# First loads cut finer, a first tile turned in halves, and a transpose queue and a TensorE order set anew

## The chip, the cores and the metric

One core of a Trainium2 chip runs the whole program. The metric is the time on the device in microseconds; lower is better. Several runs of a kernel are given as their median.

## The reference

The input x has 2048 tokens of width 448. It is normalised per token, and two branches run on the result. One is attention with a feature map: q, k and v for 16 heads of width 28, a small matrix w_phi per head, softmax of the plus and of the minus product as features, then keys times values summed over all tokens. The other is a dense pair with silu between. Both are added to x.

```python
xn = _layernorm(x, axis=-1)
qkv = (xn @ wqkv)                                # 448 -> 3*448, 16 heads of 28
pq, pk = q @ w_phi, k @ w_phi                    # per head, 28 x 28
phi = concat(softmax(p), softmax(-p))            # 56 features, for q and for k
kv, z = phi_k^T @ v, sum(phi_k)                  # over all 2048 tokens
attn = ((phi_q @ kv) / (phi_q @ z + 1e-6)) @ wo
ffn = silu(xn @ w1) @ w2                         # 448 -> 1792 -> 448
out = x + attn + ffn
```

## The kernel before

The program is a list of operations (`P.op`, `P.dma`), each with an engine, an estimated length, and what it reads and writes. `schedule` (line 218) is a planner: it simulates the engines with these estimates and fixes the order of instructions on each engine. `chain` (line 869) adds order by name where the author wants one, and the words of `PLAN` (line 334) fix TensorE's order from the fourth FFN1 block on: each word hangs on the one before. What an instruction truly waits for at run time is only its data, by semaphores.

Tokens are 16 tiles of 128. For each tile `ln_tile` (line 596) issues on VectorE the statistics (`bnst`, `bnag`), the inverse deviation (`rstd`, with a square root `ve` on ScalarE for tiles 0 to 3 and on GpSimd for the others), and the normalised tile (`xn`). Tiles 0 to 3 are turned over by four TensorE transposes each (`tr`) and evicted to `xnT` (`ev`, ScalarE for 0 to 2, VectorE for 3). Tiles 4 to 15 are turned over by DMA, two tiles at a time (`xnT_dma5`, `xnT_dma7` and so on), issued from SyncE.

The weights of q and k are folded with w_phi on the chip. Eight DMA transposes (`wT_dma0` to `wT_dma7`) bring wqkv into `wT_sb` (in the profile Y_sb, whose memory it shares), GpSimd spreads w_phi to a block diagonal (`bdphi`), and the two words f0 and f2 multiply them, each for two of four row slices. Every f word reads all eight transposes.

SyncE issues all loads in order and then the transposes: x tile 0, x tile 1, x tiles 2 and 3, w1 columns 0 to 511 and 512 to 1023 (each as three row groups and a remainder), x tiles 4 to 7, the rest of w1, wv, x tiles 8 to 11, x tiles 12 to 15, then the chain at line 910, then w2 and wo. ScalarE issues w_phi as its first instruction. `w1_sb` lies in `phT` in the profile, xn and phq in RA, the attention outputs in vaug.

The head of TensorE's order is 38 warm-up matmuls, the transposes of tiles 0 to 3, and FFN1 blocks F0, F1 and F2 (256 columns of w1 each) for tokens 0 to 511, tile by tile with 128-row matmuls (`part`). Blocks after that are done as two halves with 64-row matmuls side by side: in `PLAN` aF3@4 is the first half of FFN1 block 3 in banks 4 and 5, bF3 its second half and eviction; v, k, q are the projections of a pair of tiles. F7 and above need tiles 4 to 7. K is keys times values, Y and F with a colon are FFN2 steps of a tile, U the attention product, W, R, r and E the product with wo and the output. The kernel's own estimates list a clash of 225 ns where a half follows the other half on the same bank, and 95 ns for a switch between 64 and 128 rows.

Of the kernel before, what the change touches and what calls it, by code (L numbers as in the profile page):

```python
# [140 lines left out]
class _Prog:  # L141
# [68 lines left out]
    def dma(self, fn, xfer, reads=(), writes=(), name="", out_slot=None, eng="sp", issue=480.0, lat=1700.0):  # L210
        o = self.op(eng, issue, fn, reads, writes, name=name)
        o.is_dma = True
        o.xfer = xfer
        o.lat = lat
        o.out_slot = out_slot
        return o

    def schedule(self):
# [21 lines left out]
        eng_free = {e: 800.0 if e == "sp" else 0.0 for e in ENGINES}  # L240
# [93 lines left out]
PLAN = """aF3@4 aF4@0 bF3 aF5@2 av2@6 bF4 bv2 bF5 aF6@0 bF6 av0@4 bv0 aF7@0 aF8@2 aF10@4 bF8 bF10 bF7 f2@26 aF11@4 aF13@0 bF11  # L334
bF13 f0@26 aF9@4 aF12@0 bF9 av4@2 ak0@6 bv4 bF12 bk0 av6@4 av8@2 ak4@0 bv8 bk4 bv6 av14@6 ak2@2 bv14 bk2 av12@0 ak6@4
bv12 bk6 ak8@6 av10@2 ak10@0 bv10 bk10 bk8 ak12@2 ak14@4 bk12 bk14 aq4@0 Y0@6:3 Y0:2 K0-6 bq4 aq6@4 K6-8 bq6 aq0@2 aq8@0
bq0 bq8 aF15@4 Y0:9 K8-12 bF15 aF19@2 aF14@0 bF19 bF14 aF17@5 s4 aF18@3 bF17 bF18 K12-16 aF16@5 aF21@2 aF24@0 bF21 bF16
bF24 M s6 aF27@2 aF26@4 bF27 aF22@0 bF26 bF22 aF20@6 aq2@2 bF20 aF23@0 aF25@4 bF23 bF25 bq2 U4 s8 F4@1:10 U9@0 s0 aq12@6
aq14@4 aq10@2 s2 bq12 bq10 bq14 F4:3 F4:1 F9@0:10 F8@3:3 F8:3 s10 W4 U8 s12 F8:6 Y1@4:14 F9:4 W9 U2 U0@5 F2@2:6 F2:8
F8:2 U7@6 U12@5 W8 Y3@4:9 Y3:5 W2 s14 W0@5 F7@4:9 F7:1 U1 F7:4 W7 R0,2 R8,7 R4,9 F10@6:5 U6@5 U10 F10:9 U3@3 F5@4:14  # L340
U13@2 F15@51:8 U15 F15:6 F12@2:5 F12:9 U14 F6@0:5 W12 E15 U5 F13@3:11 F6:9 F14@7:5 F13:2 F13:1 U11@1 W5 W3@5 r12 W13
F14:9 W14 r14 W6 W1@2 W10 R3,6,13,1,5,10 F11@1:7 F11:6 F11:1 W11 r11"""


def bass_parallel_sum__linear_kernel_hedgehog__dense_activation_silu__prompt_kernel(
# [30 lines left out]
    with es:  # L376
# [157 lines left out]
        def load_rows4(dst, src, c0, c1, name, lat=1700.0):  # L534
            load(dst[:, 0:3, :], src[0:KF, c0:c1].rearrange("(k p) f -> p k f", p=128), name, lat=lat)
            load(dst[:, 3, :], src[D - 128:D, c0:c1], name, lat=lat)

        def load_w1(c0, c1, lat=1700.0):
            load_rows4(w1_sb[:, :, c0:c1], B_w1, c0, c1, "w1", lat)

        load(Wp[:], A_w_phi.rearrange("(g hl) d f -> (hl d) g f", g=G), "wphi", eng="act", lat=3000.0)
# [15 lines left out]
        def dma_t(dst, src, xfer, name, issue=1235.0, **kw):  # L557
            o = P.dma(lambda e: e.dma_start_transpose(out=dst, in_=src), xfer, lat=650.0, reads=[src] if kw.pop("sbuf", True) else [],
                      writes=[dst], name=name, issue=issue if xfer < 1500.0 else 2000.0, **kw)
# [36 lines left out]
        def ln_tile(t):  # L596
# [16 lines left out]
            def norm(dst, c0, c1, dur):  # L613
                P.op("dve", dur, lambda e: e.tensor_scalar(dst, x_sb[:, t, c0:c1], mv[:, t, 0:1], rstd[:, t:t + 1], ALU.subtract, ALU.mult),  # L614
                     reads=[xs, mv[:, t, 0:1], rstd[:, t:t + 1]], writes=[dst], name=f"xn{t}")
# [488 lines left out]
```

The softmax here doesn't subtract the row's maximum and nothing guards it: scores larger than these inputs give would overflow.

## Time and profile before

| | |
|---|---|
| median of the runs | 151.64 us (4 runs, 151.1 to 152.54) |
| profiled execution, own time | 151.12 us |
| its span, first to last instruction | 149.4 us |
| granted TensorE clock | 1.00 |
| TensorE busy | 143.9 us, 96% of the span |
| VectorE, ScalarE, GpSimd busy | 91.3, 70.2 and 70.9 us |
| first FFN1 matmul | starts at 7.05 us |
| first fold | starts at 26.28 us |
| last matmul work ends, last store lands | about 146.6 us, about 149 us |

Times in the views count from the start of the span. PE is TensorE's matmuls, PEld its weight loads, DVE VectorE, ACT ScalarE, POOL GpSimd, SP SyncE; SPq and ACTq are instructions that only issue a DMA. L468 is the helper that records every matmul, L488 the one of every ScalarE activation, so those groups are told apart by the tiles they write and read.

### The profile page before, as it was taken

To read this page: it belongs to the slowest core of one execution; us is meant where nothing else is said; L and a number is where in the kernel's file an instruction comes from. 1 tells how busy PE (TensorE), PEld (TensorE's weight loads), DVE (VectorE), ACT (ScalarE), POOL (GpSimd) and SP (SyncE) were. 2 spreads that over 40 slices of the span, in tenths; PEclk is the share of its full clock that TensorE was granted. 3 is DMA by queue.
4 is the path that set the end of the run, shared out by engine and by line. 5 is a ranking of instruction groups with operands and counts; after the bars stand their busy time and mean duration, and the time that the engine had idled before them with its cause. 6 is when DMAs were issued, how large, how long until landed. Compare 5 with 4: busy or idle time off the path is not lost.

```text
span 149.4 us, 3406 instructions
## 1 busy us (share of the span) xinstructions
PE 143.9 (96%) x1412; PEld 79.0 (53%) x1412; DVE 91.3 (61%) x186; ACT 70.2 (47%) x86; POOL 70.9 (47%) x82
## 2 busy tenths in 40 slices
PE   7699999999999999999999999999999999999992
PEld 7494434555555565454544445455555566655540
DVE  1968998850198999212995028897542974334263
ACT  3467764547999997965475495910000000000000
POOL 7208568210049999999699900999600000000000
PEclk9999999999999999999999999999999999999999
DMA  5999976999300000000099594079968645140224
GB/s 87 306 375 367 183 135 117 191 232 347 101 0 4 0 4 4 0 4 0 0 105 181 99 181 75 0 140 174 122 130 162 172 101 107 36 100 4 68 92 154
DMA packets 44352, 17.41 MB, mean 117 GB/s; under 512 B 36784, under 2 KB 43952, under 8 KB 44336
## 3 DMA queue, kind: packets, MB, share of 16 engines
q1 hardware_dynamic: 41568, 15.36, 48.1%
q10 hardware_dynamic: 2768, 1.83, 3.8%
q8 instruction: 11, 0.18, 0.5%
q14 instruction: 5, 0.04, 0.1%
HBM read 6.56 MB, written 1.84 MB: 56 GB/s over the span
## 4 chain that ended last, share of the span: by engine, by line
PE 93%; DMA 3%; SPq 1%; DVE 0%; issue 0%
PE psum L468 93%; DMA phT<-in_B_w_dram 3%; SPq L529 1%; DVE x_sb L842 0%; PE psum L483 0%
## 5 line engine op out<-in xcount | busy, mean ns | idle before, releaser
L468 PE MATMUL psum<-xnT,phT 64*128 64x512 bf16 (+1 forms) x428 | 45.1, 350 | 0.9 <-DMA phT<-in_B_w_dram 0.8
L468 PE MATMUL psum<-w_sb,hT 128*128 128x448 bf16 (+1 forms) x238 | 45.4, 342 | 0.0
L488 ACT ACTIVATE hT<-psum 128x1024 bf16<-128x1024 f32 x28 | 27.4, 1023 | 18.0 <-PE psum L468 18.0
L728 DVE TENSOR_REDUCE Rec<-Ek_sb 128x32 f32<-128x896 bf16 (+1 forms) x20 | 24.3, 1247 | 13.7 <-ACT Ek_sb L488 7.9
L468 PEld LDWEIGHTS psum<-xnT,phT 64*128 64x128 bf16 (+1 forms) x428 | 20.9, 95 | 21.5 <-ACT xnT L488 0.9
L468 PEld LDWEIGHTS psum<-w_sb,hT 128*128 128x128 bf16 x238 | 21.6, 98 | 19.0 <-issue 1.5
L763 POOL TENSOR_TENSOR RA<-Ek_sb,Rec 128x896 bf16<-128x896 bf16 x16 | 26.6, 1699 | 9.1 <-ACT Ek_sb L488 7.8
L468 PE MATMUL psum<-Wqk,xnT 64*128 64x432 bf16 x224 | 22.9, 343 | 0.0
L488 ACT ACTIVATE Ek_sb<-psum 128x864 bf16<-128x864 f32 x24 | 20.3, 934 | 2.9 <-issue 2.7
L738 POOL TENSOR_TENSOR Ek_sb<-Ek_sb,Rec 128x896 bf16<-128x896 bf16 x8 | 13.3, 1695 | 11.2 <-DVE Rec L729 11.2
L820 DVE TENSOR_SCALAR den<-psum 128x16 f32<-128x16 f32 x16 | 2.5, 162 | 22.3 <-PE psum L468 22.3
L468 PEld LDWEIGHTS psum<-Wqk,xnT 64*128 64x128 bf16 x224 | 10.6, 94 | 9.5 <-ACT Ek_sb L488 0.2
L738 POOL TENSOR_TENSOR phT<-phT,Rec 128x896 bf16<-128x896 bf16 x8 | 13.3, 1697 | 0.0
L468 PE MATMUL psum<-wv,xnT 64*128 64x448 bf16 x112 | 12.9, 349 | 0.1
L599 DVE BATCH_NORM_STATS2 st<-x_sb 128x6 f32<-128x448 bf16 x16 | 9.7, 605 | 3.9 <-DMA x_sb<-in_A_x_dram 3.8
L614 DVE TENSOR_SCALAR RA<-x_sb,mv,rstd 128x384 bf16<-128x384 bf16 (+2 forms) x28 | 10.6, 417 | 1.3 <-POOL rstd L610 1.2
L468 PE MATMUL psum<-wo_sb,vaug 128*128 128x448 bf16 (+2 forms) x51 | 11.0, 341 | 0.0
L827 DVE TENSOR_TENSOR vaug<-psum,rden 128x448 bf16<-128x448 f32 x16 | 9.9, 624 | 0.4
L842 DVE TENSOR_TENSOR x_sb<-psum,x_sb 128x448 bf16<-128x448 f32 (+2 forms) x14 | 7.6, 585 | 3.8 <-PE psum L468 3.8
L729 DVE RECIPROCAL Rec<-Rec 128x32 f32<-128x32 f32 (+1 forms) x24 | 8.6, 393 | 0.1
L468 PEld LDWEIGHTS psum<-wv,xnT 64*128 64x128 bf16 x112 | 5.4, 94 | 5.6 <-PE psum L468 0.5
L488 ACT ACTIVATE vaug<-psum 128x896 bf16<-128x896 f32 x8 | 7.4, 947 | 1.6 <-PE psum L468 1.6
(49 smaller groups left out, 102.8 us busy)
## 6 DMA issues: line engine op xcount, KB each, us to landing
out_dram<-x_sb ACTq DMA_DIRECT2D x15, 112.0 KB, 1.7
w_sb<-in_B_w_dram SPq DMA_DIRECT2D x1, 1568.0 KB, 7.8
x_sb<-in_A_x_dram SPq DMA_DIRECT2D x3, 448.0 KB, 7.5
phT<-in_B_w_dram SPq DMA_DIRECT2D x2, 384.0 KB, 4.9
wo_sb<-in_A_wo_dram SPq DMA_DIRECT2D x2, 336.0 KB, 8.9
phT<-in_B_w_dram SPq DMA_DIRECT2D x1, 576.0 KB, 6.8
wv<-in_A_wqkv_dram SPq DMA_DIRECT2D x1, 336.0 KB, 7.1
phT<-in_B_w_dram SPq DMA_DIRECT2D x2, 128.0 KB, 4.8
```

Of the source, the lines that this page charges most:

```text
L468: r = e.matmul(dst, lhsT, rhs, start=st, stop=sp, skip_group_check=True)
L488: P.op("act", d_act(n), lambda e: e.activation(dst, src, func, scale=scale), reads=[src], writes=[dst], table=table, name=name, **keys)
L529: P.dma(lambda e: e.dma_start(out=dst, in_=src), n / 280.0, writes=[dst], name=name, eng=eng, lat=lat)
L599: P.op("dve", 590, lambda e: e.bn_stats(st6[:, t, :], xs), reads=[xs], writes=[st6[:, t, :]], name=f"bnst{t}", okeys_w=["ln"])
L614: P.op("dve", dur, lambda e: e.tensor_scalar(dst, x_sb[:, t, c0:c1], mv[:, t, 0:1], rstd[:, t:t + 1], ALU.subtract, ALU.mult), reads=[xs, ...
L728: P.op("dve", 50 + 967 * n, lambda e: e.tensor_reduce(R2, E4, AXL.X, ALU.add), reads=[E4], writes=[R2], name="Ssum")
L729: P.op("dve", 135 + 210 * n, lambda e: e.reciprocal(R2, R2), reads=[R2], writes=[R2], name="Rrec")
L738: P.op("pool", 1700, lambda e: e.tensor_tensor(E3, E3, Rk[:, :, None].broadcast_to([128, 32, DH]), ALU.mult), reads=[E3, Rk], writes=[E3], ...
L763: P.op("pool", 1700, lambda e: e.tensor_tensor(dst, Eq, Rq.rearrange("p (c j) -> p c j", c=CC)[:, :, :, None].broadcast_to([128, CC, 4, DH ...
L820: P.op("dve", 190, lambda e: e.tensor_scalar(den[:, uq, :], U3[:, :, DH], EPS_DEN, None, ALU.add), reads=[U3[:, :, DH]], writes=[den[:, uq ...
L827: P.op("dve", 620, lambda e: e.tensor_tensor(o3, U3[:, :, 0:DH], rden[:, uq, :, None].broadcast_to([128, H, DH]), ALU.mult), reads=[U3[:, ...
L842: P.op("dve", d_dve(cs.stop - cs.start), lambda e: e.tensor_tensor(res[:, cs], ob, addend[:, cs], ALU.add), reads=[ob, addend[:, cs]], wri ...
```

## The change

- w1 comes in pieces of 256, 256, 256, 512 and 512 columns in place of 512, 512 and 768. The first piece is issued by ScalarE, after its first activation (`warm_act`); the others by SyncE. w_phi moves from ScalarE's first place to SyncE's queue, behind x tiles 12 to 15.
- Tile 0 is normalised in two parts (256 and 192 columns), transposed in two parts, and evicted in two parts. F0 and F1 take the first two row slices of tile 0 before the third, and F2 comes before tile 1.
- On SyncE's queue x tiles 12 to 15 and w_phi stand behind `xnT_dma5`, and `wT_dma3` to `wT_dma7` stand behind `xnT_dma7`.
- GpSimd's two memsets of the ones column wait for the last normalisation (xn15) in place of following rstd15 in order.
- The planner's estimates for DMA issue and transfer change, and `PLAN` has a new order of the same blocks. In its first line aF6 and aF5 come before the v blocks, bF4 follows bF3, f0 comes before f2, and aF8 stands ahead of bv0.

```diff
-    def dma(self, fn, xfer, reads=(), writes=(), name="", out_slot=None, eng="sp", issue=480.0, lat=1700.0):
+    def dma(self, fn, xfer, reads=(), writes=(), name="", out_slot=None, eng="sp", issue=520.0, lat=1700.0):
...
-        eng_free = {e: 800.0 if e == "sp" else 0.0 for e in ENGINES}
+        eng_free = {"sp": 800.0, "act": 2550.0, "pe": 0.0, "dve": 0.0, "pool": 0.0}
...
-PLAN = """aF3@4 aF4@0 bF3 aF5@2 av2@6 bF4 bv2 bF5 aF6@0 bF6 av0@4 bv0 aF7@0 aF8@2 aF10@4 bF8 bF10 bF7 f2@26 aF11@4 aF13@0 bF11
-bF13 f0@26 aF9@4 aF12@0 bF9 av4@2 ak0@6 bv4 bF12 bk0 av6@4 av8@2 ak4@0 bv8 bk4 bv6 av14@6 ak2@2 bv14 bk2 av12@0 ak6@4
...
+PLAN = """aF3@4 aF4@0 bF3 bF4 aF6@6 aF5@2 bF6 bF5 av2@4 bv2 av0@6 aF8@2 aF7@0 bF8 aF10@4 bv0 bF10 bF7 f0@26 aF11@4 aF13@0 bF11
+bF13 f2@26 aF9@4 aF12@0 bF9 av4@2 ak0@6 bv4 bF12 bk0 av8@2 av6@4 ak4@0 bv8 bk4 bv6 av14@6 ak2@2 bv14 bk2 av12@0 ak6@4
...
-        def load_rows4(dst, src, c0, c1, name, lat=1700.0):
-            load(dst[:, 0:3, :], src[0:KF, c0:c1].rearrange("(k p) f -> p k f", p=128), name, lat=lat)
-            load(dst[:, 3, :], src[D - 128:D, c0:c1], name, lat=lat)
-
-        def load_w1(c0, c1, lat=1700.0):
-            load_rows4(w1_sb[:, :, c0:c1], B_w1, c0, c1, "w1", lat)
-
-        load(Wp[:], A_w_phi.rearrange("(g hl) d f -> (hl d) g f", g=G), "wphi", eng="act", lat=3000.0)
+        def load_rows4(dst, src, c0, c1, name, eng="sp"):
+            load(dst[:, 0:3, :], src[0:KF, c0:c1].rearrange("(k p) f -> p k f", p=128), name, eng)
+            load(dst[:, 3, :], src[D - 128:D, c0:c1], name + "r", eng)
+
+        def load_w1(c0, c1, eng="sp"):
+            load_rows4(w1_sb[:, :, c0:c1], B_w1, c0, c1, f"w1_{c0}", eng)
+
         load_x(0, 1)
         load_x(1, 2)
         load_x(2, 4)
-        load_w1(0, 512)
-        load_w1(512, 1024)
+        load_w1(0, 256, "act")
+        load_w1(256, 512)
+        load_w1(512, 768)
         load_x(4, 8)
-        load_w1(1024, FF)
+        load_w1(768, 1280)
+        load_w1(1280, FF)
         load_rows4(wv_sb, A_wqkv, 2 * D, 3 * D, "wv")
         load_x(8, 12)
         load_x(12, 16)
+        load(Wp[:], A_w_phi.rearrange("(g hl) d f -> (hl d) g f", g=G), "wphi", lat=2500.0)
...
-                dma_t(wT_sb[:, a, :], A_wqkv[:, a * KP:a * KP + 128], 600.0, f"wT_dma{a}", (1600.0, 1400.0, 1780.0, 3280.0)[a] if a < 4 else 1300.0, sbuf=False)
+                dma_t(wT_sb[:, a, :], A_wqkv[:, a * KP:a * KP + 128], 600.0, f"wT_dma{a}", 1800.0 if a == 2 else 1310.0, sbuf=False)
...
                 if t % 2:
                     dma_t(xnT[:, t - 1:t + 1, :, :].rearrange("p i k c -> p (i k) c"),
-                          xn_sb[:, sl - 1:sl + 1, :].rearrange("p i c -> p (i c)"), 1300.0, f"xnT_dma{t}", 1350.0)
+                          xn_sb[:, sl - 1:sl + 1, :].rearrange("p i c -> p (i c)"), 2200.0 if t < 8 else 1600.0, f"xnT_dma{t}", 1350.0)
                 return
-            tps = bank16[4 + t % 2][:, 0:512].rearrange("p (k c) -> p k c", k=4)
-            transposes([(tps[:, kt, :], xn_sb[:, sl, KS[kt]:KS[kt] + 128]) for kt in range(4)], f"tr{t}")
-            if t < 3:
-                act(dstx, tps, ACTF.Identity, 512, f"ev{t}")
+
+            def turn_over(k0, k1, b, tag):
+                tps = bank16[b][:, 128 * k0:128 * k1].rearrange("p (k c) -> p k c", k=k1 - k0)
+                transposes([(tps[:, kt - k0, :], xn_sb[:, sl, KS[kt]:KS[kt] + 128]) for kt in range(k0, k1)], f"tr{tag}")
+                if t < 3:
+                    act(dstx[:, k0:k1, :], tps, ACTF.Identity, 128 * (k1 - k0), f"ev{tag}")
+                else:
+                    copy(dstx[:, k0:k1, :], tps, 128 * (k1 - k0), f"ev{tag}")
+
+            if t == 0:
+                norm(xn_sb[:, sl, 0:256], 0, 256, 290, "a")
+                norm(xn_sb[:, sl, 256:D], 256, D, 275)
+                turn_over(0, 2, 4, "0a")
+                turn_over(2, 4, 5, "0")
             else:
-                copy(dstx, tps, 512, f"ev{t}")
-
-
+                norm(xn_sb[:, sl, 0:D], 0, D, 390)
+                turn_over(0, 4, (4, 5, 4)[t - 1], str(t))
...
-            def part(c0, c1):
+            def part(c0, c1, steps=(0, 1, 2)):
                 for i in range(2):
-                    for n, kt in enumerate((0, 1, 2 + i)):
+                    for n, kt in ((n, (0, 1, 2 + i)[n]) for n in steps):
                         mm(banks[b0 + i][:, c0:c1], lhs(i, kt, slice(0, 128)), rhs(i, kt, slice(0, 128), c0, c1),
                            n == 0 and c0 == 0, False, name)
...
-                      1300.0 * w, "phqT")
+                      (1900.0, 2500.0)[w - 1], "phqT", (1250.0, 2000.0)[w - 1])
...
-        chain("bnst0 bnag0 bnst1 bnag1 rstd0 xn0 rstd1 xn1 bnst2 bnag2 bnst3 bnag3 rstd2 xn2 rstd3 xn3 ev3".split())
-        chain("ev0 ve2 ev1 ve3 ev2 silu_table".split())
-        chain("tr0 tr1 tr2 tr3".split())
+        chain("bnst0 bnag0 bnst1 bnag1 rstd0 xn0a xn0 rstd1 xn1 bnst2 bnag2 bnst3 bnag3 rstd2 xn2 rstd3 xn3 ev3".split())
+        chain("warm_act w1_0 w1_0r ve0 ve1 ev0a ev0 ve2 ev1 ve3 ev2 silu_table".split())
+        chain("tr0a tr0 tr1 tr2 tr3".split())
...
         head = [F(0, 0), F(1, 2), F(2, AUX)]
-        for t, fs in ((0, head[:2]), (1, head[:2]), (0, head[2:]), (1, head[2:]), (2, head), (3, head)):
-            for f in fs:
+        for f, steps in ((0, (0, 1)), (1, (0, 1)), (0, (2,)), (1, (2,)), (2, (0, 1, 2))):
+            head[f][0](0, 128, steps)
+        for t in range(1, 4):
+            for f in head:
                 f[0](t * 128, t * 128 + 128)
...
-        chain("wT_dma0 wT_dma1 wT_dma2 wT_dma3 xnT_dma5 wT_dma4 xnT_dma7 wT_dma5 wT_dma6 wT_dma7 xnT_dma9 xnT_dma11 xnT_dma13 xnT_dma15 w2 "
+        chain("x8 wT_dma0 wT_dma1 wT_dma2 xnT_dma5 x12 wphi xnT_dma7 wT_dma3 wT_dma4 wT_dma5 wT_dma6 wT_dma7 xnT_dma9 xnT_dma11 xnT_dma13 xnT_dma15 w2 "
               "wo0 wor0 wo1 wor1".split())
-        late = next(o.id for o in P.ops if o.name == "rstd15")
+        late = max(o.id for o in P.ops if o.name == "xn15")
         ones_column(0, NEK)
         ones_column(NEK, NT)
         for o in P.ops[-2:]:
-            o.odeps.add(late)
+            o.deps.add(late)
```

## The prediction

> **What bounds the kernel now.** I read the page first (busy shares, then the chain that ended last), then the chain as a list in order of time, then the timelines of the first 30 us, and last the DMA queue of SyncE. The page:
>
> ```profile
> PE 143.9 (96%) x1412; PEld 79.0 (53%) x1412; DVE 91.3 (61%) x186; ACT 70.2 (47%) x86; POOL 70.9 (47%) x82
> ...
> PE 93%; DMA 3%; SPq 1%; DVE 0%; issue 0%
> ```
>
> TensorE is the bound. No other engine passes 61%. The list of the chain says where the chain is not TensorE (start us, length us, what):
>
> ```profile
> 2.19 4.73 DMA phT<-in_B_w_dram
> 6.92 0.14 issue
> 7.05 1.16 PE psum L468 x18
> ...
> 13.08 0.04 issue
> 13.12 6.05 PE psum L468 x56
> 19.17 0.05 issue
> 19.21 1.62 PE psum L468 x14
> 20.84 0.05 issue
> 20.89 125.73 PE psum L468 x1204
> 146.62 0.02 issue
> 146.64 0.62 DVE x_sb L842
> ```
>
> The reader is to see three things. Real work begins at 7.05, released by a load of w1 (phT and w1 share memory) that landed at 6.92. From 20.89 to 146.62 TensorE runs 1204 matmuls without a gap, so no wait ends late there. And three small breaks lie at 13.08, 19.17 and 20.84; in the matmul starts each costs 0.21 to 0.23 us beyond the stream time. So a change can shorten the head, take out those breaks, shorten the work itself, or add waits. Nothing else moves the end.
>
> **The work itself does not change.** I summed both plans by words: 49 block halves of each kind, 2 folds, 16 U, 15 W, 224 FFN2 steps with the same one tile split over two banks, and ten slots of the last Wo row (before: R words with three and three pairs, E15 and three r words; after: the same count). Both have 20 switches between 64-row and 128-row matmuls, each 98 ns in the trace (starts 0.31 apart where 0.21 is streaming). The Trainium skill, "TensorEngine Tiling (Array Packing)", Key Properties, says that a change of tiling mode drains TensorE; the trace agrees with that 98 ns. No gain and no loss here. The tail is the same too: the last word is one r, then an eviction of 0.62 us and a store.
>
> **What the skill says of the rest.** "DMA: Bandwidth & Descriptors", Issuing engines are not separate DMA queues: transfers started by ScalarE and SyncE run on the same 16 engines, and a second issuer saves only issue time. No run here shows it for these loads yet, but DMA share is 0.99 at 5.4 to 7.05 us, so there is no idle bandwidth to win. Same page, Why small descriptors are slow: a fixed cost per packet. The trace agrees: 896 B packets take 42 ns, 1024 B 47, 1792 B 75, 3584 B 141, which is about 9 ns plus 0.037 ns per byte. A w1 piece of 256 columns has 512 B rows, so an estimate of 28 ns each, 56 for 1024 B instead of 47. "SBUF — State Buffer", Who interferes with whom: a DVE instruction in a two-port mode and a GpSimd instruction block each other for a whole instruction. The trace shows a normalisation of tile 15 stretched to 2.29 us beside GpSimd's memsets:
>
> ```profile
> L614 DVE TENSOR_SCALAR RA<-x_sb,mv,rstd x28: 296/364/2294, 4.9 to 27.1; 128x384 bf16<-128x384 bf16 x12, 128x128 bf16<-128x128 bf16 x12, 128x448 bf16<-128x448 bf16 x4
> ```
>
> Making those memsets wait for xn15 removes 1.9 us from DVE, but xn15 feeds only the last transpose, which TensorE needs after 40 us. GpSimd's next work is then at 43.19. Worth nothing.
>
> **The head, step by step.** Loads: before, F0 and F1 wait for w1 columns 0 to 511. After, F0 needs only columns 0 to 255. ScalarE loses the w_phi issue (0.41 us) but still runs its table load and warm_act (ends 2.75) before it issues w1_0, by about 3.2 with the row remainder. First packets come 1.1 us after an issue (x0: 0.80 to 1.9), so from 3.8 it shares the engines with x2 and w1_256. Bytes say that F0's piece lands at about 5.6 to 6.2.
> Tile 0: xn0 starts at 4.90. The half of 256 columns takes about 0.30 instead of 0.40, two transposes instead of four save 0.11, the eviction of 256 columns takes about 0.39 instead of 0.60. Transposed data is there at about 6.0 instead of 6.47. So TensorE can begin at about 6.15, 0.9 earlier.
> That 0.9 is not kept. F0 to F2 on tile 2 wait for ev2, and ev2 hangs on DVE's serial chain:
>
> ```profile
> 5.41 0.40 DVE L614 TENSOR_SCALAR RA<-x_sb,mv,rstd 128x448 bf16<-128x448 bf16 x1
> ...
> 5.93 0.63 DVE L599 BATCH_NORM_STATS2 st<-x_sb 128x6 f32<-128x448 bf16 x1
> ...
> 8.48 0.60 ACT L488 ACTIVATE xnT<-psum 128x512 bf16<-128x512 bf16 x1 [0.65 <-PE psum L483]
> ```
>
> The split of xn0 adds some 0.09 on DVE (two fixed costs), so the statistics of tile 2 can't start before about 5.85 even if x2 comes early: ev2 ends at 9.0 to 9.1 as before. TensorE reached tile 2 at 7.05 + 44 x 0.056 = 9.51 (36 head matmuls and 8 transposes). After, it reaches it at about 9.15. The head gains 0.36, not 0.9.
>
> **The two clashes.** The breaks at 19.17 and 20.84 are a half followed at once by the other half of its own block (aF6 bF6, av0 bv0 in the plan). The new order has one such pair ahead of the fold (av2 bv2): gain 0.23. The break at 13.08 is F4 waiting for the eviction of F0, and the new order begins with the same two words: nothing.
>
> So TensorE would come to the first fold 0.59 earlier. The timeline of TensorE before, from F7 on:
>
> ```profile
> 21.65 4.70 PE L468 MATMUL psum<-xnT,phT 64*128 64x512 bf16 x42
> 26.28 0.96 PE L468 MATMUL psum<-BDphi,Y_sb 112*128 112x112 bf16 x16
> ```
>
> The fold starts at 26.28; after, it could at 25.69.
>
> **The transposes on SyncE's queue.** Here the gain meets a wait. The fold needs all eight wT transposes.
>
> ```profile
> 8.39 6.80 SPq L558 DMA_TRANSPOSE Y_sb<-in_A_wqkv_dram  x4
> 15.23 1.31 SPq L558 DMA_TRANSPOSE xnT<-RA  x1
> 16.58 1.27 SPq L558 DMA_TRANSPOSE Y_sb<-in_A_wqkv_dram  x1
> 17.89 1.31 SPq L558 DMA_TRANSPOSE xnT<-RA  x1
> 19.24 3.90 SPq L558 DMA_TRANSPOSE Y_sb<-in_A_wqkv_dram  x3
> ...
> DMA to landing us min/median/max: 3.3/4.8/8.0
> ```
>
> Before, wT7 is issued at 21.88 and lands at 25.52, 0.76 ahead of its use. After, the queue is 15 loads (one more), wT0 to wT2, xnT_dma5, x12, wphi, xnT_dma7, then five wT in a row. The loads end at about 8.9. wT0 to wT2 take 1.3 + 1.3 + 1.4 to 1.8 and end by 13.4. xnT_dma5 waits for xn5 (DVE, about 13.3, bnst4 being 0.45 earlier with x4) and, I take it, for room in the queue as wT3 did, to about 15.0. x12 and wphi 1.1, so xnT_dma7 from 16.1 to 17.5. Five wT at 1.3: wT7 is issued at about 22.7, 0.8 later than before. Landing takes 3.3 (least) to 3.6 (wT7 before): 26.0 to 26.3, and I take 26.1. TensorE is there at 25.69 and waits 0.4. The fold starts at about 26.1, so 0.2 earlier than before, and from there all is as before.
> xnT_dma7 is used by F8 at 21.65 - 0.76 - 0.36 - 0.23 = 20.3 (F8 now stands ahead of bv0's 0.76). It was issued at 17.89 and landed at 21.49; from 16.1 it lands at 19.7 to 20.2. Its bounds are 0 and 0.5 of wait, and the fold's wait takes either in. w_phi's product (0.93 us on GpSimd) has from 19 to 25.7: nothing, unless w_phi is over 5 us late. x12 lands near 18.5, ahead of DVE's use at 19.6.
> Later waits: the phi products on GpSimd end at 69.7 and K12-16 starts at 71.1, and the new plan places it 0.65 later: nothing.
>
> **Sum.** -0.36 - 0.23 + 0.4 = about -0.2 us. The profiled execution took 151.12 (span 149.4), so 150.9 for it; the median of the runs shown is 151.64, 0.5 above, so 151.4. A change under 1% (1.5 us) is about what a measurement of this kernel can't tell from none.
>
> **Rivals.**
> (A) The forecast, fold bound by wT7: -0.4 to +0.3. Chance 0.45.
> (B) Everything lands in time, and head and clash are kept, with x0 a little earlier without w_phi beside it: -0.5 to -0.9, so 150.9. For it: xnT_dma5 may be issued without a stall, which would bring wT7 to 25.6. Chance 0.25.
> (C) Slower: SyncE's queue. If xnT_dma5 blocks for as long as wT3 did (2.76 instead of 1.31, 4 transposes in 6.80), wT7 is issued at 24.1 and lands at 27.6 (3.5) to 28.5 (4.4, as wT6 took before): the fold starts 1.4 to 2.2 later, so about 153.4. It decides as soon as wT7 lands after 26.3, and passes 1% after 27.8. Against it: wT3 waited behind x12, which is now behind. Chance 0.17.
> (D) The loads don't do what they say: w1_512 is third, and before the x2 packets took up to 1.46 us each at the start. On an engine that ends x2 at 5.6, 96 packets of 28 ns end at 8.3, landing 8.6. F2's tile 0 then comes at 8.65 and tile 2 at 10.45, 0.94 later; less the clash, +0.7, so 152.3. Chance 0.13.
>
> **The numbers.** Likeliest is A: 151.4. The range reaches from B's low end with the scatter of the runs, 150.4, to 153.0, which leaves out most of C. Faster by over 1% needs 1.5 us, and the head can't give it: 0.09, for scatter. Slower by over 1%: C mostly, and waits that I don't see in a new order of 130 us: 0.19. Within 1%: 0.72.
>
> **What would show it.** First FFN1 matmul at about 6.2, tile 2 at 9.1 to 9.2, one break of 0.23 before the fold, the first fold at 26.0 to 26.3 with a wait on the Y_sb transposes, then TensorE unbroken to about 146.0. A fold at 25.7 without a wait means B, at 27.5 or later C, a head that reaches tile 2 after 9.5 means D. A new gap after 30 us would be outside this account.

## The result: slightly slower, and the profile after

| | before | changed |
|---|---|---|
| median of the runs made together | 152.24 us (63 runs, 151.06 to 154.88) | 152.92 us (42 runs, 151.65 to 155.29) |
| ratio to before, 95% interval | | 1.0043 [1.0027, 1.0060] |
| profiled execution, own time (span) | 151.12 (149.4) us | 154.13 (152.4) us |

The change costs 0.4%, about 0.65 us, where 0.2 us of gain was forecast. The profiled execution of the changed kernel is one of its slow ones, 1.2 us above its median; a second profile of the same program (153.12 us, below) stands beside it where a size matters.

The page of the changed kernel, busy shares and the chain that ended last:

```profile
PE 144.4 (95%) x1412; PEld 79.5 (52%) x1412; DVE 89.5 (59%) x187; ACT 70.4 (46%) x87; POOL 70.8 (46%) x82
...
PE 79%; SPq 9%; DMA 7%; DVE 2%; issue 1%
```

TensorE does the same work (144.4 us against 143.9), but only 79% of the chain is TensorE, against 93%. SyncE's issues and DMA have taken the rest. The list of the chain, its middle and end (start us, length us, what):

```profile
8.77 7.67 DMA x_sb<-in_A_x_dram
...
23.19 2.48 SPq L560
25.67 0.04 issue
25.71 3.46 DMA Y_sb<-in_A_wqkv_dram
29.17 0.14 issue
29.30 120.33 PE psum L468 x1154
```

Before, the last unbroken stretch of TensorE began at 20.89. Here it begins at 29.30, with the first fold, released by the eighth transpose of wqkv, issued at 25.71 and landed at 29.17. TensorE's timeline up to there (start, length, what, in brackets the idle time before and what ended it):

```profile
6.83 0.83 PE L468 MATMUL psum<-xnT,phT 128*128 128x128 bf16 x12
...
18.88 2.29 PE L468 MATMUL psum<-wv,xnT 64*128 64x448 bf16 x20
22.14 2.98 PE L468 MATMUL psum<-xnT,phT 64*128 64x512 bf16 x26 [0.97 <-issue]
24.95 0.94 PE L468 MATMUL psum<-wv,xnT 64*128 64x448 bf16 x8
25.70 1.91 PE L468 MATMUL psum<-xnT,phT 64*128 64x512 bf16 x16
29.30 0.95 PE L468 MATMUL psum<-BDphi,Y_sb 112*128 112x112 bf16 x16 [1.69 <-DMA Y_sb<-in_A_wqkv_dram]
```

Two waits are new. F8 begins at 22.14, right after xnT_dma7 landed at 22.05 (by matmul starts it lost 1.14 us; the view puts its 0.97 down to "issue"). The fold then waits 1.7 us for wT7. The head begins at 6.83, where 7.05 was measured before and 6.15 was forecast. In the second profile (after_again) only the second wait is left:

```profile
22.22 2.97 PE L468 MATMUL psum<-xnT,phT 64*128 64x512 bf16 x26
...
28.30 0.95 PE L468 MATMUL psum<-BDphi,Y_sb 112*128 112x112 bf16 x16 [0.62 <-DMA Y_sb<-in_A_wqkv_dram]
```

There TensorE itself comes to F8 later, for a reason shown under "The clock". SyncE's queue in the first profile, where both waits come from:

```profile
8.77 0.47 SPq L529 DMA_DIRECT2D x_sb<-in_A_x_dram  x1
9.28 4.91 SPq L560 DMA_TRANSPOSE Y_sb<-in_A_wqkv_dram  x3
14.30 2.26 SPq L560 DMA_TRANSPOSE xnT<-RA  x1
16.60 0.58 SPq L529 DMA_DIRECT2D x_sb<-in_A_x_dram  x1
17.23 0.43 SPq L529 DMA_DIRECT2D Wp<-in_A_w_phi_dram  x1
17.71 1.26 SPq L560 DMA_TRANSPOSE xnT<-RA  x1
19.01 7.96 SPq L560 DMA_TRANSPOSE Y_sb<-in_A_wqkv_dram  x5
```

**One number carries the whole time.** From the first fold's start to the last matmul's start it is 119.97 us in the kernel before and in the changed one, and in every kernel below but three. Own time less the start of the first fold is therefore nearly a constant: 151.12 - 26.28 = 124.84 before, 154.13 - 29.30 = 124.83 after. So the new order of TensorE's work costs and gains nothing behind the fold, and the question is only when the fold starts. If that holds in the executions whose traces were not kept, the medians, read backwards, give an estimate of where it starts in a usual one: 152.24 - 124.83 = 27.4 before and 152.92 - 124.83 = 28.1 after. The profile of before that the forecast was made from, with its fold at 26.28 and no wait, was an execution 1.1 us below the median.

### The profile page after: what moved, and what is told of

Its sections match the earlier page's. It is cut to its first block, busy times and chain, and to the rows that moved or that the text cites. A ratio compares the mean times of both kernels' runs of the same rounds, so it can differ in the third digit from the quotient of the medians.

```text
span 152.4 us, 3415 instructions
## 1 busy us (share of the span) xinstructions
PE 144.4 (95%) x1412; PEld 79.5 (52%) x1412; DVE 89.5 (59%) x187; ACT 70.4 (46%) x87; POOL 70.8 (46%) x82
## 4 chain that ended last, share of the span: by engine, by line
PE 79%; SPq 9%; DMA 7%; DVE 2%; issue 1%
PE psum L468 79%; DMA x_sb<-in_A_x_dram 5%; SPq L529 5%; SPq L560 4%; DMA Y_sb<-in_A_wqkv_dram 2%; DVE st L601 1%; DVE x_sb L850 0%; DVE mv L602 0%; DVE RA L616 0%
## 5 line engine op out<-in xcount | busy, mean ns | idle before, releaser
L488 ACT ACTIVATE hT<-psum 128x1024 bf16<-128x1024 f32 x28 | 27.4, 1022 | 16.8 <-PE psum L468 16.8
L746 POOL TENSOR_TENSOR Ek_sb<-Ek_sb,Rec 128x896 bf16<-128x896 bf16 x8 | 13.3, 1696 | 10.7 <-DVE Rec L737 10.7
L746 POOL TENSOR_TENSOR phT<-phT,Rec 128x896 bf16<-128x896 bf16 x8 | 13.3, 1696 | 0.0
L616 DVE TENSOR_SCALAR RA<-x_sb,mv,rstd 128x384 bf16<-128x384 bf16 (+4 forms) x29 | 8.9, 348 | 2.6 <-POOL rstd L612 2.4
```

Source lines behind the costliest of these rows:

```text
L488: P.op("act", d_act(n), lambda e: e.activation(dst, src, func, scale=scale), reads=[src], writes=[dst], table=table, name=name, **keys)
L746: P.op("pool", 1700, lambda e: e.tensor_tensor(E3, E3, Rk[:, :, None].broadcast_to([128, 32, DH]), ALU.mult), reads=[E3, Rk], writes=[E3], ...
```

## The experiments

Ratios are to the kernel before, run on the same chip, with 95% intervals. "Fold" is the start of the first fold in the one profiled execution; its wait, in brackets, is by matmul starts and so 0.06 to 0.07 us more than in the views. "Tile 2" is the start of the first head matmul on tile 2. Landings are the last of the arrivals that the trace has for a transfer.

| kernel | ratio | profiled: own time | tile 2 | x4 landed | xnT_dma7 landed | wT7 issued, landed | fold (wait) |
|---|---|---|---|---|---|---|---|
| before, given | | 151.12 | 9.51 | 9.93 | 21.49 | 21.88, 25.52 | 26.28 (0) |
| before_again | 0.9989 [0.9960, 1.0018] | 151.78 | 9.16 | 9.70 | 22.23 | 22.34, 26.15 | 26.96 (0) |
| after, given | 1.0043 [1.0027, 1.0060] | 154.13 | 9.86 | 10.54 | 22.05 | 25.71, 29.17 | 29.30 (1.76) |
| after_again | 1.0034 [1.0009, 1.0060] | 153.12 | 11.06 | 10.12 | 21.34 | 24.87, 28.16 | 28.30 (0.69) |
| queue_only | 0.9974 [0.9947, 1.0002] | 151.71 | 9.53 | 10.17 | 20.41 | 22.47, 26.50 | 26.85 (0.54) |
| loads_only | 1.0069 [1.0035, 1.0103] | 153.08 | 9.65 | 10.28 | 23.38 | 23.72, 28.02 | 28.26 (0.15) |
| plan_old | 1.0032 [1.0005, 1.0059] | 151.49 | 9.88 | 9.82 | 20.97 | 23.40, 26.37 | 26.66 (0) |
| loads_old | 0.9992 [0.9962, 1.0021] | 151.85 | 9.39 | 10.07 | 21.07 | 23.02, 26.89 | 27.03 (0.47) |
| queue_old | 1.0159 [1.0107, 1.0211] | 153.97 | 9.66 | 10.37 | 23.63 | 23.83, 27.85 | 29.12 (0) |
| queue_mid | 1.0011 [0.9986, 1.0036] | 151.99 | 9.70 | 9.77 | 19.98 | 23.81, 27.02 | 27.16 (0.92) |
| keep_wt3 | 1.0043 [1.0022, 1.0065] | 152.46 | 11.08 | 10.13 | 21.89 | 23.12, 27.07 | 27.62 (0) |
| one_queue | 1.0131 [1.0072, 1.0190] | 153.42 | 10.20 | 11.59 | 22.69 | 25.79, 28.45 | 28.58 (0.40) |
| wphi_first | 0.9966 [0.9943, 0.9988] | 151.09 | 9.59 | 9.03 | 20.53 | 22.55, 26.11 | 26.24 (0.12) |
| wphi_first_again | 0.9915 [0.9899, 0.9931] | 152.02 | 10.27 | 9.22 | 20.83 | 23.03, 27.06 | 27.20 (0.39) |
| wphi_act_late | 1.0001 [0.9976, 1.0025] | 153.63 | 11.08 | 10.09 | 22.38 | 24.57, 28.64 | 28.78 (0.91) |

**The same programs again.** after_again and before_again are unaltered.

> The changed kernel once more, unaltered, to see a second profiled execution. Theory T (transposes): TensorE unbroken from the first fold on, and ahead of it a wait of F8 for xnT_dma7 and a wait of the fold for wT7, together 1 to 3 us; the fold starts 0.5 to 1 us later than before (26.8 to 27.3), wT7 is issued after 23.5. Rival L (loads): the first FFN1 matmuls are late because the finer loads land late, and tile 2 is reached after 9.6; the fold then waits little. Ratio to before 1.002 to 1.007 under both.

> The kernel before, unaltered, for a second profiled execution. Theory C (clock): the runs of the kernel before fall in two groups, near 151.3 and near 152.4, because in some executions the head's 128-column matmuls run at 107 ns each in place of 56; if this profile is of the slower group, tile 2 is reached 1.1 us later (about 10.7) and the fold starts near 27.4 with no wait for wT7; otherwise 26.3. Ratio 0.998 to 1.002.

The loss is confirmed (1.0034). The two profiles differ in own time by 153.12 - 151.78 = 1.34, and in the fold by 28.30 - 26.96 = 1.34: the whole difference lies ahead of the fold. In its profile the kernel before waits too, as TensorE's timeline shows:

```profile
22.32 4.71 PE L468 MATMUL psum<-xnT,phT 64*128 64x512 bf16 x42 [0.84 <-issue]
26.96 0.96 PE L468 MATMUL psum<-BDphi,Y_sb 112*128 112x112 bf16 x16
```

F7 stands until xnT_dma7 lands, at 22.23. So in this execution before is bound by SyncE's queue as well, at another of its transposes, and a queue that brings xnT_dma7 earlier has something to win.

**The parts one by one.** queue_only is before with the new order of transposes, loads_only is before with the new loads (w_phi on SyncE behind x12), plan_old is the changed kernel with the old order of TensorE, loads_old the changed kernel with the old loads (w_phi first on ScalarE), queue_old the changed kernel with the old order of transposes.

```diff
# queue_only, on before
-chain("wT_dma0 wT_dma1 wT_dma2 wT_dma3 xnT_dma5 wT_dma4 xnT_dma7 wT_dma5 wT_dma6 wT_dma7 xnT_dma9
+chain("x8 wT_dma0 wT_dma1 wT_dma2 xnT_dma5 x12 xnT_dma7 wT_dma3 wT_dma4 wT_dma5 wT_dma6 wT_dma7 xnT_dma9
# queue_old, on after
-chain("x8 wT_dma0 wT_dma1 wT_dma2 xnT_dma5 x12 wphi xnT_dma7 wT_dma3 wT_dma4 wT_dma5
+chain("x8 x12 wphi wT_dma0 wT_dma1 wT_dma2 wT_dma3 xnT_dma5 wT_dma4 xnT_dma7 wT_dma5
```

> The kernel before with only the new order of transposes: x tiles 12 to 15 behind xnT_dma5, wT3 and wT4 behind xnT_dma7; loads (w_phi first from ScalarE), whole tile 0 and plan stay old. Theory P: the wait for xnT_dma7 goes, wT7 is issued at 23.0 to 23.8 and lands at 26.5 to 27.2, fold at 26.7 to 27.3, ratio 0.998 to 1.003. Rival R: 1.003 to 1.007.

> The kernel before with only the new loads: w1 in five pieces, the first from ScalarE, w_phi on SyncE behind x tiles 12 to 15; transposes and plan stay old. Theory P (every issue on SyncE ahead of the transposes counts): wT0 starts 1 to 2 us later than in the kernel before, xnT_dma7 lands at 22.5 to 23.7 and F7 waits 1 to 2 us for it, fold at 27.5 to 28.8, ratio 1.006 to 1.012. Rival R (the loads are neutral, the loss is the reordered queue): ratio 0.998 to 1.002.

> The changed kernel with TensorE's old order. Theory P: the fold waits for wT7 in any order, so only F7's later place is felt and covered by that wait; ratio 1.002 to 1.006, fold to last matmul 119.97 us as in both. Rival: the new order itself costs, ratio 0.998 to 1.001.

> The changed kernel with the old loads: w1 in pieces of 512, 512 and 768 columns from SyncE, w_phi first from ScalarE. Halves of tile 0, the order of the transposes (x tiles 12 to 15 behind xnT_dma5) and TensorE's order stay as changed. Theory T: the loads end about 0.5 us earlier and so does the queue, a small gain, ratio to before 1.000 to 1.004. Rival L: the whole loss goes, tile 2 is reached at 9.2 to 9.5, ratio 0.995 to 0.999.

> The changed kernel with SyncE's old order of transposes: x tiles 12 to 15 and w_phi ahead of wT0, wT3 ahead of xnT_dma5, wT4 ahead of xnT_dma7. Loads, halves and TensorE's order stay as changed. Theory T: if the new queue order is what makes the fold late, wT7 lands 0.7 to 1.2 us earlier and the kernel gains 0.4 to 0.8 us on the changed one, ratio to before 0.997 to 1.001, although F8 waits longer for xnT_dma7 (up to 1 us). Rival L: the queue waits for the loads whatever its order, ratio stays 1.003 to 1.007.

Behind the new queue the order of TensorE's work is neutral: with the old one the changed kernel still stands at 1.0032, inside the interval of the whole. The new queue alone does not lose, 0.9974 with an interval that just includes 1. The loads alone lose 0.7%, and with the old queue in the otherwise changed kernel, where a gain had been expected, the loss is 1.6%. So the loss comes with the loads, and the new queue takes most of it back. SyncE's queue in loads_only says how:

```profile
7.00 1.79 SPq L529 DMA_DIRECT2D wv<-in_A_wqkv_dram  x2
8.83 0.97 SPq L529 DMA_DIRECT2D x_sb<-in_A_x_dram  x2
9.85 0.70 SPq L529 DMA_DIRECT2D Wp<-in_A_w_phi_dram  x1
10.59 6.46 SPq L560 DMA_TRANSPOSE Y_sb<-in_A_wqkv_dram  x4
17.09 1.31 SPq L560 DMA_TRANSPOSE xnT<-RA  x1
```

The first transpose starts at 10.59 in place of 8.39, and everything behind it shifts: xnT_dma7 lands at 23.38 and TensorE stands 1.67 us, by matmul starts, ahead of F7. In queue_old the same wait is 2.75 in the view, ahead of F8:

```profile
23.72 2.98 PE L468 MATMUL psum<-xnT,phT 64*128 64x512 bf16 x26 [2.75 <-issue]
```

wT7 is not what binds here: it landed at 27.85, and the fold starts at 29.12 without a wait. That the old queue costs more with the new order of TensorE (1.0159) than with the old one (loads_only, 1.0069) has a reason in the traces: from F8 to the fold it is 29.12 - 23.72 = 5.40 us, since bv0 now stands behind F8, and from F7 to the fold before it was 26.28 - 21.65 = 4.63. A wait for xnT_dma7 so late puts the fold off by 0.77 more.

**Single moves on SyncE's queue.** queue_mid puts x12 ahead of the transposes and w_phi on ScalarE behind w1's first piece; keep_wt3 moves wT3 back ahead of xnT_dma5; x12_last moves x12 behind wT7; mix1 does both moves of the last two with the old loads.

```diff
# queue_mid, on after (and wphi behind w1_0r in ScalarE's chain)
+chain("x8 x12 wT_dma0 wT_dma1 wT_dma2 xnT_dma5 xnT_dma7 wT_dma3 ...
# keep_wt3, on after
+chain("x8 wT_dma0 wT_dma1 wT_dma2 wT_dma3 xnT_dma5 x12 wphi xnT_dma7 wT_dma4 ...
# x12_last, on after
+chain("x8 wT_dma0 wT_dma1 wT_dma2 xnT_dma5 wphi xnT_dma7 wT_dma3 ... wT_dma7 x12 xnT_dma9
# mix1, on loads_old
+chain("x8 wT_dma0 wT_dma1 wT_dma2 wT_dma3 xnT_dma5 xnT_dma7 wT_dma4 ... wT_dma7 x12 xnT_dma9
```

> The changed kernel with x tiles 12 to 15 ahead of wT0 and w_phi issued by ScalarE behind the first piece of w1, so that nothing but transposes stands between wT0 and wT7; xnT_dma5 and xnT_dma7 still go ahead of wT3. Theory T: 1.0 us of SyncE's issue time leaves the stretch, but the bytes of x move ahead of the transposes; wT7 lands about 0.5 us earlier, ratio to before 0.998 to 1.003. Rival L: 1.003 to 1.007.

> The changed kernel with one transpose put back: wT3 goes ahead of xnT_dma5 again, all else as changed. Theory S: SyncE stands idle from about 13.4 to 14.6 us because xnT_dma5 waits for the normalisation of tile 5 with five wT behind it; wT3 fills that time, wT7 is issued about 1 us earlier (near 23.9), the fold starts 0.5 to 1 us earlier, ratio to before 0.997 to 1.001. Rival B: the bytes of the loads ahead set when any transpose can move, the issue order does not matter, ratio 1.002 to 1.006.

> The changed kernel with x tiles 12 to 15 moved from behind xnT_dma5 to behind wT7. Theory S: 0.6 us of issue and 1.3 us of transfer leave the stretch; xnT_dma7 lands about 1 us earlier, wT7 0.6 to 1.3 us earlier, ratio to before 0.996 to 1.001. Rival B: same direction, since the bytes leave too, but the fold follows the bytes (1.3 us) and not the issue.

> The old loads (w1 in 512, 512, 768 columns from SyncE, w_phi first from ScalarE), wT3 ahead of xnT_dma5, x tiles 12 to 15 behind wT7; halves of tile 0 and TensorE's new order stay. Theory S: tile 2 at 9.3 to 9.4, xnT_dma7 lands by 20.3, wT7 by 25.5, so neither wait is left and the fold starts at 25.8 to 26.1, ratio to before 0.995 to 0.998. Rival B: the transposes still start when the loads have landed and the fold stays at 26.8 or later, ratio 0.999 to 1.002.

x12_last has its fold early, at 26.43, and loses 1.6% all the same: 1.0164 [1.0114, 1.0213]; mix1 (fold at 26.15) stands at 1.0090 [1.0054, 1.0126]. These are two of the three kernels in which the stretch from fold to last matmul is not 119.97: 122.40 and 123.14 (the third, "best" below, has 120.27). TensorE and SyncE of x12_last:

```profile
35.01 0.74 PE L468 MATMUL psum<-wv,xnT 64*128 64x448 bf16 x6 [1.29 <-DVE Wqk L594]
36.48 0.72 PE L468 MATMUL psum<-Wqk,xnT 64*128 64x432 bf16 x6 [0.73 <-DVE Wqk L594]
```

```profile
24.60 0.59 SPq L529 DMA_DIRECT2D x_sb<-in_A_x_dram  x1
25.23 11.40 SPq L560 DMA_TRANSPOSE xnT<-RA  x4
```

x12 landed at 28.70 and VectorE normalises its four tiles ahead of the eviction of the second fold (Wqk), so TensorE waits there, by matmul starts 1.46 + 0.91 us; the last four xnT transposes stretch over 11.40 us instead of 5.50. So x12 can't move to the end for nothing: what it gains ahead of the fold, it more than loses behind it. keep_wt3 does bring wT7 earlier in its profile, issued at 23.12 and landed at 27.07, and its fold at 27.62 waits for TensorE alone, which came late to tile 2 (11.08, see "The clock"); still the kernel as a whole stands at 1.0043. queue_mid, which takes w_phi off SyncE and brings xnT_dma7 at 19.98, stands at 1.0011, too near after_again's 1.0034 to call it a gain. keep_wt3, x12_last and mix1 had been expected at 0.995 to 1.001, and all three missed.

**The first load from one queue.** one_queue issues w1's first piece from SyncE, behind x tiles 2 and 3.

```diff
-        load_w1(0, 256, "act")
+        load_w1(0, 256)
```

> The changed kernel with the first piece of w1 issued by SyncE behind x tiles 2 and 3, in place of ScalarE. Theory Q: the second queue put w1's first packets ahead of x tile 1, which lands at 4.4 in place of 3.65 and holds VectorE's chain 0.3 to 0.4 us; here x tile 1 lands at 3.6 to 3.8 and tile 2 is reached at 9.2 to 9.4 (changed kernel 9.66 to 9.86), but two more issues on SyncE put every transpose about 1 us later, so the fold is later: ratio to before 1.004 to 1.010. Rival: x tile 1 is late for another reason and tile 2 stays at 9.6 or later.

VectorE in one_queue, and in the changed kernel, at the point where tile 1 arrives and tile 0 is normalised:

```profile
3.71 0.59 DVE L601 BATCH_NORM_STATS2 st<-x_sb 128x6 f32<-128x448 bf16 x1
...
4.61 0.59 DVE L616 TENSOR_SCALAR RA<-x_sb,mv,rstd 128x256 bf16<-128x256 bf16 x2
```

```profile
4.36 0.63 DVE L601 BATCH_NORM_STATS2 st<-x_sb 128x6 f32<-128x448 bf16 x1 [0.35 <-DMA x_sb<-in_A_x_dram]
...
5.29 0.59 DVE L616 TENSOR_SCALAR RA<-x_sb,mv,rstd 128x256 bf16<-128x256 bf16 x2
```

With w1_0 off ScalarE tile 1 lands at 3.36 and not at 4.34, and the normalisation of tile 0, queued behind tile 1's statistics, starts 0.68 earlier. FFN1 starts at 6.29. So the second issuer does press on x, as had been expected. But FFN1 then waits for w1 (0.86 us after its fifth matmul), tile 2 is reached at 10.20, where 9.2 to 9.4 had been expected, and SyncE has two more issues: 1.0131. Both places for w1_0 have a price.

**The clock.** In after_again the head's matmuls start 107 ns apart, not 56, until about 9.9 us (a "cold" head), with a granted clock of 1.00:

```profile
7.13 2.13 PE L468 MATMUL psum<-xnT,phT 128*128 128x128 bf16 x18
```

That is 18 matmuls in 2.13 us, where the given profile has 12 in 0.83. The Trainium skill ("TensorE: Matmul & The Clock Gate", Part 1: The HAM clock gate) states 106.7 ns for a cold array and 55.6 for a warm one, and that the switch depends on where in a free-running window the work falls; the traces agree with both numbers, and no run here shows the window. Three kernels add six warm-up matmuls and six fillers in the head's idle stretch: before_warm, after_warm, and "best", which is before_warm with both clashes also taken out of the plan (aF6 av0 bF6 bv0 in place of aF6 bF6 av0 bv0, and aF8 ahead of aF7).

```diff
-        for i in range(38):
+        for i in range(44):
...
+            if t == 1:
+                fill(6)        # six 128-column matmuls on a spare bank
```

> The kernel before with 44 warm-up matmuls in place of 38 and six more between the transposes of tile 1 and F0, so that TensorE stands idle less before the head. Theory C: fewer executions have the slow head, the median falls by 0.4 to 0.8 us, ratio 0.995 to 0.998. Rival: the two groups come from something else (loads), ratio 0.999 to 1.002.

> The changed kernel with the same 44 warm-ups and six more behind the transposes of tile 0. Theory T and C together: a faster head runs into the wait for wT7, so less comes back than in the kernel before with the same edit: 0 to 0.4 us, the fold at 27.5 to 28.3 with a wait of 1 us or more, ratio to before 1.001 to 1.004. Rival: the loss of the changed kernel is only a slow head more often, then the ratio falls to 0.996 to 0.999.

> The kernel before with the warm-ups of before_warm and a plan without the two clashes ahead of the fold (aF6 av0 bF6 bv0, F8 ahead of F7). The clashes are worth 0.46 us, less a wait of up to 0.3 us for xnT_dma7 where the head is fast: 0.15 to 0.45 us on top of before_warm, ratio 0.992 to 0.997.

0.9994 [0.9961, 1.0028], 1.0029 [1.0003, 1.0054] and 0.9985 [0.9955, 1.0015]: nothing that can be told from the same kernels without the fillers. Taking out the clashes is worth nothing that shows, either, where 0.15 to 0.45 us had been expected.

The loss doesn't need a cold head: after and after_warm have warm ones, and their folds stand at 29.30 and 27.66 with a wait for wT7 (1.69 and 0.42 in the views). But a cold head is not harmless. It costs 1.2 us at tile 2 (11.06 against 9.86), and it reaches SyncE's queue by way of VectorE: the eviction of tile 3 (ev3) comes late, and the statistics of tile 4 stand behind it. In the three profiles with a cold head (after_again, keep_wt3, wphi_act_late) these start at 10.84 to 10.88, 0.75 us after x4 has landed, and xnT_dma5 hangs on them. All three are among the ten profiles in which w1's first piece goes ahead of everything on ScalarE; none of the other ten has a cold head. Whether the change makes a cold head more frequent, and how much of the loss that is, stays open, and so does the spread of before, whose two profiles both have a warm head.

**w_phi.** The last three runs leave SyncE's order as in the change except that w_phi is issued by ScalarE: as its first instruction (wphi_first, timed twice), or behind both parts of w1_0 (wphi_act_late).

```diff
-        load(Wp[:], A_w_phi.rearrange("(g hl) d f -> (hl d) g f", g=G), "wphi", lat=2500.0)
+        load(Wp[:], A_w_phi.rearrange("(g hl) d f -> (hl d) g f", g=G), "wphi", "act", lat=2500.0)
-        chain("warm_act w1_0 w1_0r ve0 ...
+        chain("wphi warm_act w1_0 w1_0r ve0 ...        # wphi_first
+        chain("warm_act w1_0 w1_0r wphi ve0 ...        # wphi_act_late
```

> The changed kernel with w_phi back as ScalarE's first instruction, and nothing else. Theory P: one issue of 0.45 to 0.5 us leaves the stretch between xnT_dma5 and wT7, the fold comes 0.4 to 0.5 us earlier, ratio 0.999 to 1.002. Rival R: nothing changes, 1.003 to 1.005.

> The changed kernel with w_phi issued by ScalarE as its first instruction, as before the change; a second timing of it. If the first timing (0.9966 of before) was no accident: 0.994 to 0.999 of before, wT7 issued near 22.5 and landed near 26.1, first fold near 26.2 with a wait of at most 0.2. If it was an accident of that batch: 1.000 to 1.005.

> The changed kernel with w_phi issued by ScalarE behind both parts of the first w1 piece; SyncE's queue then holds the same instructions in the same order as with w_phi first on ScalarE. Theory 1 (only the issue between two transposes on SyncE cost time): the same as with w_phi first, ratio 0.995 to 0.999, wT7 landed 26.0 to 26.4. Theory 2 (w_phi's place among the first loads counts too: w1's first piece ahead of it presses on x, so x4 lands after 10 and the issues of the loads stay slow): wT0 starts after 9.1, wT7 lands at 26.8 to 27.5, the fold at 26.9 to 27.6, ratio 1.000 to 1.003.

wphi_first is faster than both kernels: 0.9966 [0.9943, 0.9988] and 0.9915 [0.9899, 0.9931], where the changed kernel's intervals begin at 1.0009 and 1.0027. It differs from the changed kernel in w_phi's move alone, so that move is the cause of the loss: the least step between the two, 1.0034 - 0.9966 = 0.7%, is more than the 0.5% by which the two timings of wphi_first differ. (Whether wphi_first is better than queue_only, 0.9974 [0.9947, 1.0002], can't be told from its first timing.)

The move has two sides, and wphi_act_late, with the same SyncE order, parts them: it stands between, at 1.0001 [0.9976, 1.0025]. Beside the second timing of wphi_first, in the same set of runs, w_phi's place on ScalarE is worth 152.00 - 151.22 = 0.8 us of the medians, and the intervals don't touch; beside the first timing, of another set, it is 152.00 - 151.50 = 0.5, and they overlap. The two timings of the one program lie further apart than their intervals, so this size is rough. Taking the issue off SyncE is worth the step from the changed kernel (1.0034 to 1.0043, in other sets) to 1.0001, 0.3 to 0.4% or 0.5 to 0.6 us; that is no more than two sets can differ by, so it is not shown by the times. The profiles do show an issue less: 0.68 us from the end of xnT_dma5's issue to xnT_dma7's, in place of 1.15.

SyncE and TensorE in wphi_first:

```profile
8.59 3.85 SPq L560 DMA_TRANSPOSE Y_sb<-in_A_wqkv_dram  x3
13.01 2.21 SPq L560 DMA_TRANSPOSE xnT<-RA  x1
15.26 0.58 SPq L529 DMA_DIRECT2D x_sb<-in_A_x_dram  x1
15.89 1.25 SPq L560 DMA_TRANSPOSE xnT<-RA  x1
17.18 7.16 SPq L560 DMA_TRANSPOSE Y_sb<-in_A_wqkv_dram  x5
```

```profile
20.74 2.97 PE L468 MATMUL psum<-xnT,phT 64*128 64x512 bf16 x26
23.55 0.92 PE L468 MATMUL psum<-wv,xnT 64*128 64x448 bf16 x8
24.30 1.89 PE L468 MATMUL psum<-xnT,phT 64*128 64x512 bf16 x16
26.25 0.95 PE L468 MATMUL psum<-BDphi,Y_sb 112*128 112x112 bf16 x16
```

F8 and the fold both go without a wait in the view, and wT7 landed at 26.11, where the forecast for the change had 26.1. The second profile of wphi_first, an execution 0.8 us above its median, has its fold at 27.20 with a wait of 0.39.

How w_phi's place on ScalarE acts is in part open. In wphi_first (first fence) and wphi_act_late (second) the statistics of tile 4 and the last of tile 5's normalisation, on VectorE:

```profile
9.29 0.62 DVE L601 BATCH_NORM_STATS2 st<-x_sb 128x6 f32<-128x448 bf16 x1
...
12.39 0.60 DVE L616 TENSOR_SCALAR RA<-x_sb,mv,rstd 128x384 bf16<-128x384 bf16 x2
```

```profile
10.50 0.42 DVE L492 COPY xnT<-psum 128x512 bf16<-128x512 bf16 x1 [1.80 <-PE psum L483]
10.84 0.62 DVE L601 BATCH_NORM_STATS2 st<-x_sb 128x6 f32<-128x448 bf16 x1
...
13.93 0.60 DVE L616 TENSOR_SCALAR RA<-x_sb,mv,rstd 128x384 bf16<-128x384 bf16 x2
```

SyncE issued xnT_dma5 0.03 us after xn5 ended, at 13.01 and at 14.56. Only part of this difference can be x4. It landed at 9.03 and at 10.09, but in wphi_act_late VectorE was held until 10.50 by TensorE, whose head was cold; that execution was 1.6 us above its kernel's median. What the other profiles add: in all ten with w1_0 ahead of everything on ScalarE x4 landed between 9.77 and 10.54, in the two with w_phi ahead of it at 9.03 and 9.22; and in the seven of the ten with a warm head the statistics of tile 4 start 0.02 to 0.03 us after x4, so there x4 is what they wait for. What wphi_act_late was expected to show, wT0 issued after 9.1, it did not: 8.68.

## Why the prediction was wrong, step by step

- **The bound, the unchanged work, the stretch behind the fold: right.** 119.97 us from the first fold in both kernels, no new gap after 30 us. Only the chain's share moved. The gain of 0.23 us from a clash less is there as well: from tile 2 to the fold, where nothing waits, it is 26.43 - 9.89 = 16.54 us with the new order (x12_last) and 26.28 - 9.51 = 16.77 before.
- **The mechanism of the forecast: right.** In all three profiles of the changed kernel, with the fillers or without (after, after_again, after_warm), the fold waits on the last wqkv transpose. Rival C had the right sign and the right place, SyncE's queue, but its cause, xnT_dma5 blocking for as long as wT3 did, was only part: that issue took 2.26 us in the given profile and 1.26 in the second. By the forecast's own sign, a fold at 27.5 or later, C is what happened; that the median is still inside the stated range, by 0.1 us, is luck and not the sum.
- **The step that failed: the sum for SyncE's queue, "wT7 issued at about 22.7", "I take 26.1".** It was issued at 25.71 and 24.87, landed at 29.17 and 28.16. The terms, for the two profiles of the changed kernel and the two with w_phi put back:

| term | forecast | after, after_again | wphi_first, again |
|---|---|---|---|
| x4 landed | (0.45 earlier than 9.93) 9.5 | 10.54, 10.12 | 9.03, 9.22 |
| xn5 done | 13.3 | 14.27, 14.56 | 12.98, 13.66 |
| xnT_dma5's issue ends | 15.0 | 16.56, 15.85 | 15.22, 15.54 |
| from there to xnT_dma7's issue (x12, w_phi) | 1.1 | 1.15, 1.15 | 0.67, 0.68 |
| xnT_dma7's issue to wT3's | 1.4 | 1.30, 1.30 | 1.29, 1.28 |
| wT3's issue to wT7's, four | 5.2 | 6.70, 6.57 | 5.37, 5.53 |
| wT7 issued | 22.7 | 25.71, 24.87 | 22.55, 23.03 |

  For after_again the excess is 0.85 + 0.05 - 0.10 + 1.37 = 2.17 us, for after 1.56 + 0.05 - 0.10 + 1.50 = 3.01. The term for x12 and w_phi itself was right. Two others were not. First, the end of xnT_dma5's issue, because xn5 was done 1.0 and 1.3 us late. In after this is x4: it landed at 10.54, and the statistics of tile 4 start at 10.57. I had moved x4 0.45 earlier (it stands one piece of w1 further up in the queue), and it came later. A load is there when its slowest part is: in the changed kernel x4's first part landed at 7.60 and its last at 10.54 (8.50 and 9.93 before). The Trainium skill, "DMA: Bandwidth & Descriptors", Why a DMA increments its semaphore by 16 and not by 1, says that the engines of one DMA finish independently and only the full count means that the data is there; the trace agrees. In after_again x4 landed at 10.12, and the cold head, which the forecast has no term for, held VectorE to 10.88. Second, "five wT at 1.3": of the issues near 21 to 25 us one takes 1.5 to 2.5 us. Before showed it (1.87 at 23.18, on xnT_dma9, where nobody waited). In after and after_again the queue was so late that the long one (2.48 and 2.31) fell ahead of wT7; in both wphi_first profiles wT7 was issued early enough to be the long one itself (1.79 and 1.90), and landed 3.6 and 4.0 us after that issue began.
- **"w_phi's product: nothing" was right, and still w_phi was the costly move**, by its issue (0.47 us in the profiles) and by leaving its place at the front of ScalarE's loads (0.5 to 0.8 us of the medians, rough). The sum has the first, inside "x12 and wphi 1.1". The second it puts at nothing, and rival B even took it for a small gain ("x0 a little earlier without w_phi beside it").
- **The head: wrong, "w1_0 by about 3.2".** I had ScalarE's table load and warm_act delay that issue. It ran beside the table load:

```profile
0.80 1.28 ACT L488 ACT_TABLE_LOAD   x1 [0.80 <-PEq L1099]
1.04 0.97 ACTq L529 DMA_DIRECT2D phT<-in_B_w_dram  x2
2.09 0.20 ACT L488 ACTIVATE warm_act<-ones_bf 128x4 f32<-128x4 bf16 x1
```

  So w1_0 was on the DMA engines from the start and took room from x tile 1 (4.34 instead of 3.65). VectorE does tile 1's statistics ahead of tile 0's normalisation, which began at 5.29 instead of 4.90. First FFN1 6.83 (forecast 6.15), tile 2 at 9.86 (forecast 9.15, before 9.51 and 9.16). Rival D had this sign but another cause. The Trainium skill, "DMA: Bandwidth & Descriptors", Issuing engines are not separate DMA queues, was cited for this in the prediction and not used for it; one_queue agrees with it: what w1_0 gained on a second issuer, x lost.
- **xnT_dma7 for F8, "19.7 to 20.2": landed at 22.05 and 21.34.** This is the same term, xnT_dma5's end. With w_phi back it came at 20.53 and 20.83.
- **The reference point.** Before was taken at 26.28 without a wait. before_again waits 1.0 us for xnT_dma7 and folds at 26.96. So part of the loss was masked: the fold of the changed kernel is 2 to 3 us later than the one forecast from, and the medians only 0.65 us apart.

## What to carry to other kernels

When work behind one point takes a constant time in all profiles, reduce every comparison to the time of that point: here the medians themselves could be read as fold starts. A queue's sum must be made from the latest arrival of each load, not from bytes, and from more than one profile: in one execution of before xnT_dma7 landed at 21.49, ahead of F7 at 21.65, and in the next F7 waited 1.0 us for it. A small load at the front of an otherwise idle issuer is not free to move: test its two prices, the issue where it goes and the order where it leaves, in separate runs; here leaving it in place gives the version to keep, wphi_first. And a cold head on TensorE can make transfers late, when an eviction that waits for it stands ahead of the next tile's work on VectorE.

## What the runs showed of the hardware that was not expected

- A DMA issue that ScalarE has behind a table load and an activation in its order ran at 1.04 us, during the table load (0.80 to 2.08) and ahead of the activation (2.09).
- In all twenty profiles a 16 KB packet of the instruction queue (the page has it as `q8 instruction`, 11 packets) starts between 21.3 and 25.5 us and takes 0.9 to 1.6 us, and a DMA transpose whose issue takes 1.5 to 2.5 us begins within 0.7 us of it. Another such packet starts at 11.8 to 13.5 us; wT3's 2.76 us at 12.42 before the change, which the forecast put down to room in the queue, began 0.10 ahead of one (12.52). That the one causes the other was not tried, so the reason for the long issues is open.
- Why w_phi ahead of w1_0 brings x4 about 1.0 us earlier (9.13 against 10.13 in the mean of two and of ten profiles) stays open: the spread of x4's parts was 1.2 us in both profiles with it and 2.0 to 2.9 in those without, but the trace does not say which engine carried what.
